# A DeltaNet + gated-GELU kernel: weight conversion that masks two pieces ahead, a new order of the second weight, wider matrix products and fills in the last solve steps

## The chip, the cores and the metric

The kernel runs on one core of one Trainium2 chip. The kernel uses five engines, with a queue of instructions each: TensorE (PE, matrix products; its weight loads are shown apart as PEld), VectorE (DVE), ScalarE (ACT), GpSimd (POOL) and SyncE (SP, which here only issues DMAs). DMAs move data between HBM (DRAM) and the on-chip memory SBUF; products are written to tiles in PSUM. The metric is the device time of one execution in microseconds (us).

## The reference

Four batches of eight heads, 768 tokens, head size 48. A delta rule runs over the tokens and its output, with the heads side by side, is the input of a two-layer block:

```python
k_n = k / (np.linalg.norm(k, axis=-1, keepdims=True) + 1e-06)
for t in range(S):
    y[:, :, t] = np.einsum('bhd,bhde->bhe', q[:, :, t], state)
    v_old = np.einsum('bhde,bhd->bhe', state, kt)
    state = state + bt[:, :, :, None] * np.einsum('bhd,bhe->bhde', kt, vt - v_old)
x = y.transpose(0, 2, 1, 3).reshape(B * S, H * D)          # 3072 x 384
h = x @ w_in                                               # 384 x 2048
out = (h * (1.0 / (1.0 + np.exp(-1.702 * h)))) @ w_out     # 2048 x 384
```

The two weights arrive in double precision (8 bytes a number); the kernel turns them into single precision itself, word by word.

## The kernel before

The tokens are cut into chunks of 128. Inside a chunk the recurrence becomes a triangular system: the Gram matrix of the keys, its diagonal 32x32 blocks inverted on VectorE (`invert`), and four block rows solved one after the other. The first chunk of all four batches (steps 0 to 3, class `Step`) is handled by `hops`: for a pair of steps a and b, eight hops alternate between "solve a block of one step" (`solve`, PSUM tile psU) and "carry the solved block to the blocks below it in the other step" (`below`, PSUM tile psV). After each hop ScalarE copies psU and then one block of psV back to SBUF (tile VU), and the next hop's products wait for both copies. `path` is the hops of steps 0 and 1, `later` those of steps 2 and 3. `put_out` then forms the outputs and the state of a step; its VectorE addition writes ST. `merge` widens 16-row inverses to 32 rows. From step 4 on (class `Half`, called from `slot`) a step has half a chunk of two batches.

The feed-forward block of two batches follows as `hidden` (tile ph, product with w_in, then the activation on ScalarE into gT) and `written` / `both_written` / `seven` (tile po, product with w_out). From step 4 on these products are mixed with the steps by `spend`, and in `later` by `feed`.

The order of each engine's queue is the order in which the Python code emits instructions (`pinned`, line 139 in the profile: nearly every instruction has this line, so tiles tell them apart). Four generators are woven in by hand:

- `conversion` turns one piece of a weight into single precision. Its six instructions are, in order: mask (VectorE, exponent bits of the high words into the destination), clamp (ScalarE), or (VectorE, adds the sign), hi (VectorE, mantissa bits), lo (VectorE, adds the low words), mul (VectorE, the final product into the destination).
- `pieces` lists the pieces: 0 to 3 are halves of the first two quarters of w_in, 4 to 6 and 7 to 9 the thirds of its last two quarters (called (2,0) to (3,2) below, 128x512 each), then the 16 row blocks f of w_out in the order of `order`, with f = 4, 5 and f = 6, 7 taken together.
- `conversions` strings them together. Before the change a piece's mask and clamp are emitted after the hi of the piece before it.
- `background` interleaves the conversions with the inversion of the second chunk, which begins when the eighth row block of w_out is done. `fill(us)` emits from it until the costs that it yields reach that many microseconds.

The raw thirds of w_in are fetched by `fetch_in` on SP's queue. `paced` lets such a fetch wait for a solved block: POOL copies one word of it into the fetch's destination. `fetches` tells which raw row blocks of w_out are fetched once a piece has been converted, since their room becomes free then: some rooms are inside the tile w_out itself (`inside`), the others are buffers of other tiles (`outside`).

`warm(n)` puts n products without use on PE (tile ps_warm), of 128x128 by 128x256 in bf16. They stand at the start, between the products of the first chunk, and in the hops of `path`.

Of the kernel before, what the change touches and what calls it, by code (L numbers as in the profile page):

```python
# [8 lines left out]
F32 = mybir.dt.float32  # L9
# [9 lines left out]
def kernel(  # L19
# [21 lines left out]
    B, H, S, D = q.shape  # L41
    DM, DFF = moe_w_in.shape
# [5 lines left out]
    KC = DM // 128  # L48
    FC = DFF // 128
    BS = 32  # L50
    NB = C // BS
    HB = 2
# [8 lines left out]
    NQ = DFF // 4  # L61
# [8 lines left out]
    ps_moe = ctx.enter_context(tc.tile_pool(name="ps_moe", bufs=2, space=PSUM))  # L70
# [80 lines left out]
    vec, act, pe, pool = Engine(nc.vector), Engine(nc.scalar), Engine(nc.tensor), Engine(nc.gpsimd)  # L151
# [16 lines left out]
    ones = ident.bitcast(mybir.dt.bfloat16)  # L168

    def warm(n, after=None):  # L170
        ps = ps_moe.tile([128, 256], F32, tag="moe", name="ps_warm")
        if after is not None:
            after(ps[:, 0:1], 0.0)
        for _ in range(n):
            pe.matmul(ps, lhsT=ones[:, 0:128], rhs=ones, start=True, stop=True)

    table = cpool.tile([128, 1], F32, name="table")
    act.activation(table, ident[:, 0:1], ACT.Gelu_apprx_sigmoid)
# [41 lines left out]
    def fetch_in(i, other=None, js=None, only=None):  # L220

        f = slice(i * NQ, (i + 1) * NQ)
        for j in range(KC) if js is None else js:
            dst = as_rows(thirds[(i - 2) * KC + j])[:, 0] if i >= 2 else as_rows(quarter(i))[:, j]
            for p, r, m, step in x_rows:
                if only is not None and p // DP != only:
                    continue
                (other if other and (p >= DP or js) else sync)(
                    out=dst[p : p + m], in_=moe_w_in[r + j * step : r + j * step + m, f]
                )  # L230

    places, slots = {}, {}
    inside = {3: 6, 4: 8, 5: 10, 6: 12, 7: 14, 12: 14, 13: 10}
    outside = {0: "xT", 8: "xT", 11: "xT", 1: "M", 9: "M", 14: "M", 2: "M2", 10: "M2", 15: "M2"}
    order = [0, 4, 5, 1, 3, 2, 6, 7, 8, 13, 9, 10, 12, 11, 14, 15]

    def fetch_out(f, dma=sync):

# [10 lines left out]
    def conversion(dst, raw, shape):  # L249

        lo, hi = raw[:, :, :, 0], raw[:, :, :, 1]
        ts, stt = vec.tensor_scalar, vec.scalar_tensor_tensor
        AND, OR = ALU.bitwise_and, ALU.bitwise_or
        E1 = 1 << 20
        p = dst.bitcast(I32)
        ts(p, hi, 0x7FF * E1, None, op0=AND)  # L260
        yield 0.75
        act.activation(p, p, ACT.Relu, scale=8.0, bias=low)
        yield 0.0
        stt(out=p, in0=hi, scalar=-(1 << 31), in1=p, op0=AND, op1=OR)
        yield 0.95
        ts(hi, hi, E1 - 1, E1, op0=AND, op1=OR)
        yield 0.7
        f = lo.bitcast(F32)
        stt(out=f, in0=lo.bitcast(U32), scalar=2.0**-32, in1=hi, op0=ALU.mult, op1=ALU.add)
        yield 0.95  # L270
        stt(out=dst, in0=f, scalar=2.0**-20, in1=dst, op0=ALU.mult, op1=ALU.mult)
        yield 0.95
# [27 lines left out]
    def conversions():  # L300

        whole = list(pieces())

        def begin(i):
            dst, raw, shape, name = whole[i]
            ops = conversion(dst, places[name[1]] if raw is None else raw, shape)
            return ops, next(ops)

        after, cost = begin(0)
        next(after)  # L310
        yield cost
        for i in range(len(whole)):
            ops = after
            yield next(ops)
            yield next(ops)
            if i + 1 < len(whole):
                after, cost = begin(i + 1)
                yield cost
                next(after)
            yield next(ops)  # L320
            cost = next(ops)
            done.add(whole[i][3])
            fetches.pop(whole[i][3], lambda: None)()
            yield cost
# [22 lines left out]
    def fill(us):  # L347
        while us > 0:
            us -= next(behind, us)

    ready = {}
    inverse = {}
# [217 lines left out]
    def send_blocks(n, others=(), dma=sync):  # L570

        G = ready[n][2]
        Nd = dram.tile([H * C * BS], F32, tag="Nd", name="Nd", bufs=4)
        to = Nd.rearrange("(h p k) -> p h k", p=C, k=BS)
        for blk in range(NB):
            u = slice(blk * BS, (blk + 1) * BS)
            k = u if n < B else slice(blk % 2 * BS, (blk % 2 + 1) * BS)
            (beside if blk in others else dma)(out=to[u], in_=G[u, :, k])
        return Nd

    def load_diagonals(Nds):

        for b in range(B):
            load_diagonal(b, Nds[b], sync)
# [88 lines left out]
    def merge(pair, area, banks):  # L673

        XT, Pm = (
            [area[:, a + i * n : a + (i + 1) * n].rearrange("p (h k) -> p h k", h=H) for i in range(HB)]
            for a, n in ((0, H * BS), (HB * H * BS, H * BS // 2))
        )
        Z, HS = [inverse[X.n] for X in pair], BS // 2
        rows = [slice(k * BS, (k + 1) * BS) for k in range(NB)]  # L680
        for X, t in zip(Z, XT):
            vec.transpose(t.rearrange("p h k -> p (h k)"), X.rearrange("p h k -> p (h k)"))
        for X, x, m in zip(pair, Z, Pm):
            ps = banks[0][0].tile([128, H, HS], F32, tag=banks[0][1], name="psP")
            for h in range(H):
                for r in rows:
                    pe.matmul(
                        ps[r, h, :], lhsT=X.G[r, h, r], rhs=x[r, h, HS:], start=True, stop=True,
                        skip_group_check=True,
                    )  # L690
            act.activation(m, ps, ACT.Copy, scale=upper)
            yield
        for x, t, m in zip(Z, XT, Pm):
            ps = banks[1][0].tile([128, H, HS], F32, tag=banks[1][1], name="psZ")
            pe.matmul(ps, lhsT=ident, rhs=x[:, :, HS:], start=True, stop=True, skip_group_check=True)
            for h in range(H):
# [16 lines left out]
    class Step:  # L713
# [69 lines left out]

        def below(self, blk, h, psR):
            r = slice(blk * BS, (blk + 1) * BS)
            for k in range(blk + 1, NB):
                u = slice(k * BS, (k + 1) * BS)
                pe.matmul(
                    self.psV[u, h, :], lhsT=self.G[r, h, u], rhs=self.U[r, h, :],
                    start=False, stop=True, skip_group_check=True,  # L790
                )
# [420 lines left out]
    def run(work):  # L1212
        for _ in work:
            pass
# [161 lines left out]
    ahead_of(inverting, 1 + BS // 2 - 1)  # L1376
    next(inverting)
    run(inverting)
    for b in range(HB, B):
        load_values(b, sync)  # L1380
    pair = [new_step(n) for n in range(B)]
# [15 lines left out]
    def paced(sign, i, j):  # L1397

        words = thirds[(i - 2) * KC + j]
        pool.tensor_copy(words[0:1, 0, 0:1, 0].bitcast(F32), sign)  # L1400
        fetch_in(i, js=(j,))
# [5 lines left out]
        warm(NM)  # L1407
    next(products)
    warm(NM)
    paced(inverse[0][0:1, 0, BS // 2 : BS // 2 + 1], 2, 0)  # L1410
    next(scaling)
    turn(B)
    run(products)
# [11 lines left out]
    def put_out(s, us=1.7):  # L1425
        s.queries()
        s.outputs(True, lambda: fill(us))
        steps.pop(s.n)

    path, later = hops(*pair[:2]), hops(*pair[2:])  # L1430
    for i in range(2 * NB):
        together(*next(path))
        if i in (0, 1, 2, 4, 6):
            at = pair[i % 2].US[i // 2 * BS : i // 2 * BS + 1, 0:1]
            paced(at, *{0: (2, 1), 1: (2, 2), 2: (3, 0), 4: (3, 1), 6: (3, 2)}[i])
        if i == 0:
            warm(NU // 2)
            run(scaling)
        if i in (0, 3, 5):
            turn(B + {0: 1, 3: 2, 5: 3}[i])  # L1440
        if i in (2, 4, 6):
            gram(B + i // 2 - 1)
        if i < 2 * NB - 1:
            warm(NU if i == 1 else NU // 2 if i else 2 * NU // 3)
        if i < 2 * NB - 2:
            fill(2.1)
    put_out(pair[0], 0)
    fetch_out(0, other_queue)
    merging = merge(pair[2:], area, ((ps_big, "big"), (ps_big, "big")))
    put_out(pair[1], 0)  # L1450
    for f in (1, 2):
        fetch_out(f, other_queue)
# [28 lines left out]
    for i in range(2 * NB):  # L1481
        if i == 0:
            for _ in range(HB):
                feed()
                next(merging)
                fill(1.5)
        together(*next(later))
        if i == 1:
            gram(B + HB + 1)
            load_diagonals([send_blocks(n) for n in range(B, 2 * B)])  # L1490
        feed()
        fill(2.3)
    for s in pair[2:]:
# [100 lines left out]
```

## Time and profile before

| | |
|---|---|
| median of 3 runs | 689.9 us (687.72 to 691.27) |
| profiled execution | 696.56 us |
| its span | 694.8 us (1.8 us lie around it) |
| mean granted TensorE clock | 0.972 |
| PE | 670.7 us busy, 9161 products and 9161 weight loads |
| DVE | 474.4 us |
| ACT | 232.0 us |
| POOL | 272.0 us |

The profiled execution is 6.7 us longer than the median of the runs. Times in the text are microseconds from the start of the span. The profile's view by stretches gives each engine's busy time and count of instructions, then the granted clock of TensorE (1.00 is full speed), the mean busy share of the DMA engines and GB/s. In the view in order of time, the bracket at the end of a row is the idle time of the engine ahead of it and what ended that.

### The profile page before, as it was taken

The numbers are of one execution on the slowest core, as the hardware profiler recorded it, in microseconds if no ns is written. First come the engines' busy times: TensorE is split into PE (matmuls) and PEld (weight loads), VectorE is DVE, ScalarE is ACT, GpSimd is POOL, SyncE is SP. The second block draws the span as 40 slices with busy tenths as digits, with TensorE's granted clock in tenths as the row PEclk, the third lists the DMA queues.
The fourth block names the chain that finished last, engine by engine and source line by source line (L and its number), as shares of the span: only waits on it lengthen the run. The fifth ranks groups of instructions, "written<-read, shape, count | busy, mean of one in ns | idle before, by whom it ended". The sixth has DMA issues, their size and how long they took to land.

```text
span 694.8 us, 21515 instructions
## 1 busy us (share of the span) xinstructions
PE 670.7 (97%) x9161; PEld 579.7 (83%) x9161; DVE 474.4 (68%) x888; ACT 232.0 (33%) x563; POOL 272.0 (39%) x290
## 2 busy tenths in 40 slices
PE   9599999998999999999999999999999999999997
PEld 7477878874568898998998998988988988989997
DVE  4787167999688999796997996997995980200000
ACT  3345445552323323323333233233233233232120
POOL 6040084531148751752643734634414305205041
PEclk9679599999999999999999999999999999999999
DMA  8995366647234435336226324335231130000101
GB/s 171 145 172 124 86 144 201 126 73 156 70 85 97 79 73 110 63 69 131 59 49 133 79 61 104 80 63 98 63 66 36 37 66 10 19 13 5 27 0 24
DMA packets 158528, 56.70 MB, mean 82 GB/s; under 512 B 146464, under 2 KB 151296, under 8 KB 158432
## 3 DMA queue, kind: packets, MB, share of 16 engines
q1 hardware_dynamic: 153888, 47.80, 34.3%
q0 software_dynamic: 3456, 7.40, 4.4%
q8 instruction: 72, 1.18, 0.7%
q10 hardware_dynamic: 1088, 0.13, 0.1%
q14 instruction: 24, 0.20, 0.1%
HBM read 39.42 MB, written 14.68 MB: 78 GB/s over the span
## 4 chain that ended last, share of the span: by engine, by line
PE 81%; DVE 6%; DMA 4%; issue 3%; SPq 2%; POOL 2%; ACT 1%; POOLq 0%; DVEq 0%; ACTq 0%
PE ph L139 31%; PE po L139 30%; PE four L139 7%; PE ps_warm L139 4%; PE psU L139 3%; SPq L139 2%; PE psR L139 2%; DVE P L139 2%; DMA KN<-in_k_dram 2%; PE psG L139 1%; DVE w_out L139 1%; DVE YB L139 1%; DMA bL<-in_beta_dram 1%; DVE NT L139 1%; DMA NT<-Nd 1%
## 5 line engine op out<-in xcount | busy, mean ns | idle before, releaser
L139 PE MATMUL ph<-xT,w_in 128*128 128x256 f32 x1152 | 259.8, 383 | 0.9 <-DMA xT<-last 0.9
L139 PEld LDWEIGHTS ph<-xT,w_in 128*128 128x128 f32 x1152 | 215.4, 190 | 31.6 <-DMA xT<-last 1.3
L1063 POOL TENSOR_TENSOR gT<-gT 128x512 f32<-128x512 f32 x80 | 103.2, 1300 | 98.7 <-ACT gT L139 66.0
L139 PE MATMUL po<-w_out,gT 128*128 128x192 f32 (+1 forms) x720 | 138.6, 348 | 0.7 <-DVE w_out L139 0.7
L139 PEld LDWEIGHTS po<-w_out,gT 128*128 128x128 f32 x720 | 118.4, 190 | 12.1 <-DVE w_out L139 1.3
L139 DVE TENSOR_TENSOR P<-NT,YB 64x8 f32<-64x8 f32 (+13 forms) x195 | 124.4, 638 | 5.6
L139 ACT ACTIVATE gT<-ph 128x512 f32<-128x512 f32 x90 | 53.7, 597 | 154.4 <-PE ph L139 153.7
L139 DVE TENSOR_REDUCE YB<-P 64x4 f32<-64x8 f32 (+13 forms) x195 | 78.4, 402 | 6.7
L139 PE MATMUL po<-TW,gT 128*128 128x192 f32 x480 | 81.8, 328 | 0.0
L139 PEld LDWEIGHTS po<-TW,gT 128*128 128x128 f32 x480 | 78.1, 190 | 0.7
L929 POOL TENSOR_SCALAR_AFFINE_SELECT M<-M 64x512 f32<-64x512 f32 x40 | 29.8, 745 | 88.3 <-ACT M L139 87.0
L139 ACT COPY VU<-psU 32x384 f32<-32x384 f32 x96 | 45.0, 469 | 27.7 <-PE psU L139 16.6
L139 DVE TENSOR_TENSOR o<-o,late 128x192 f32<-128x192 f32 x20 | 6.5, 355 | 68.0 <-ACT late L139 67.9
L139 DVE TENSOR_TENSOR VU<-VU,psR 32x384 f32<-32x384 f32 x40 | 22.1, 554 | 32.6 <-PE psR L139 31.8
L366 POOL TENSOR_TENSOR rn<-ssq,half 128x8 f32<-128x8 f32 x12 | 22.4, 1865 | 50.4 <-DVE ssq L139 50.4
L139 PEld LDWEIGHTS psU<-VU,XB 32*32 32x32 f32 x1536 | 29.6, 107 | 13.1 <-issue 8.5
L109 POOL DMA_DIRECT2D KN<-in_k_dram x24 | 17.2, 717 | 59.0 <-PE four L139 35.9
L139 ACT COPY o<-po 128x192 f32<-128x192 f32 (+1 forms) x44 | 14.7, 333 | 75.6 <-PE po L139 73.5
L139 DVE TENSOR_TENSOR VU<-VU,four 128x384 f32<-128x384 f32 x19 | 10.4, 548 | 42.7 <-ACT M L139 42.5
L139 PE MATMUL ps_warm<-ident 128*128 128x256 bf16 x225 | 35.6, 314 | 2.8 <-POOL low L139 1.4
L139 PE MATMUL psU<-VU,XB 32*32 32x48 f32 x1536 | 34.9, 206 | 1.5 <-DVE w_out L139 1.4
L139 PEld LDWEIGHTS <-ident 128*128 128x128 bf16 x225 | 23.8, 111 | 10.1 <-issue 3.0
(165 smaller groups left out, 775.5 us busy)
## 6 DMA issues: line engine op xcount, KB each, us to landing
VU<-in_v_dram SPq DMA_DIRECT2D x40, 96.0 KB, 3.1
out_dram<-o SPq DMA_DIRECT2D x40, 96.0 KB, 2.2
QW<-in_q_dram SPq DMA_DIRECT2D x76, 48.0 KB, 2.2
Kd<-KN SPq DMA_DIRECT2D x56, 64.0 KB, 2.2
late<-Kd SPq DMA_DIRECT2D x14, 256.0 KB, 2.9
NT<-Nd SPq DMA_DIRECT2D x24, 128.0 KB, 3.0
Yd<-NT SPq DMA_DIRECT2D x24, 128.0 KB, 2.3
XB<-Yd SPq DMA_DIRECT2D x24, 128.0 KB, 3.1
```

The lines of the kernel that those rows point to most:

```text
L109: dma(out=place(dst, n)[rows, :, 0:D], in_=src[b, :, t, :].rearrange("h p d -> p h d"),)
L139: return lambda *a, **kw: tc.keep_in_program_order(op(*a, **kw))
L366: nc.gpsimd.tensor_tensor(rn, ssq, half, op=ALU.pow)
L929: nc.gpsimd.affine_select(out=M, in_=M, compare_op=ALU.is_gt, fill=0.0, base=0, pattern=[[0, H], [1, CH]], channel_multiplier=-1,)
L1063: (engine or nc.gpsimd).tensor_tensor(o, a, b, op=op)
```

## The change

Six things change, all of them in or for the first 125 us of the program.

1. Dummies: `warm(n)` issues n // 2 products of 128x512 (the same 256 columns read twice) and one of 128x256 if n is odd.
2. Products: `below` of a `Step` covers the blocks 2 and 3 with one product of 64 rows of output, so that a step has 4 products a head in place of 6.
3. Conversion: the mask of a piece is emitted up to two pieces ahead where its destination does not overlap raw data that is still needed (`clear`), and its clamp one piece ahead.
4. The order of w_out's row blocks; the new order holds both for the conversion and for `both_written`.
5. Fetches: (2,0) of w_in is no longer paced; (2,1) takes its place behind `merge`, and the others follow at hops 0, 1, 3 and 5 rather than 0, 1, 2, 4 and 6.
6. Fills: `fill(2.1)` also in hops 6 and 7 and `fill(2.0)` between the two `put_out`s. The Gram blocks of steps 4 and 5 are sent to DRAM in hops 5 and 6, not all together in `later`.

```diff
     def warm(n, after=None):
-        ps = ps_moe.tile([128, 256], F32, tag="moe", name="ps_warm")
+        ps = ps_moe.tile([128, 2, 256], F32, tag="moe", name="ps_warm")
...
-        for _ in range(n):
-            pe.matmul(ps, lhsT=ones[:, 0:128], rhs=ones, start=True, stop=True)
+        twice = ones.rearrange("p (o k) -> p o k", o=1).broadcast_to([128, 2, 256])
+        for _ in range(n // 2):
+            pe.matmul(ps, lhsT=ones[:, 0:128], rhs=twice, start=True, stop=True)
+        if n % 2:
+            pe.matmul(ps[:, 0], lhsT=ones[:, 0:128], rhs=ones, start=True, stop=True)
...
-    order = [0, 4, 5, 1, 3, 2, 6, 7, 8, 13, 9, 10, 12, 11, 14, 15]
+    order = [0, 1, 3, 4, 5, 2, 6, 7, 8, 9, 13, 12, 10, 14, 11, 15]
...
+        def span(i, raw):
+            kind, f = whole[i][3]
+            if kind == "in":
+                return (4 * NQ, 6 * NQ) if raw and f == 4 * KC - 1 else (0, 0)
+            m = whole[i][2][0]
+            if not raw:
+                return f * DM, (f + m) * DM
+            return (inside[f] * DM, (inside[f] + 2 * m) * DM) if f in inside else (0, 0)
+        def clear(i, j):
+            lo, hi = span(j, False)
+            return all(hi <= a or b <= lo for a, b in (span(k, True) for k in range(i, j)))
...
-        after, cost = begin(0)
-        next(after)
-        yield cost
-        for i in range(len(whole)):
-            ops = after
+        last = len(whole) - 1
+        yield begin(0)
+        clamp(0)
+        yield begin(1)
+        for i in range(last + 1):
+            ops = begun[i]
             yield next(ops)
+            clamp(i + 1)
             yield next(ops)
-            if i + 1 < len(whole):
-                after, cost = begin(i + 1)
-                yield cost
-                next(after)
+            if i < last and i + 1 not in begun:
+                yield begin(i + 1)
+                clamp(i + 1)
+            if i + 2 < last and clear(i, i + 2):
+                yield begin(i + 2)
             yield next(ops)
...
-            for k in range(blk + 1, NB):
-                u = slice(k * BS, (k + 1) * BS)
+            for a, b in {0: ((1, 2), (2, 4)), 1: ((2, 4),), 2: ((3, 4),)}[blk]:
+                u = slice(a * BS, b * BS)
...
     run(inverting)
+    fetch_in(2, js=(0,))
     for b in range(HB, B):
         load_values(b, sync)
...
-    paced(inverse[0][0:1, 0, BS // 2 : BS // 2 + 1], 2, 0)
+    paced(inverse[0][0:1, 0, BS // 2 : BS // 2 + 1], 2, 1)
...
-        if i in (0, 1, 2, 4, 6):
+        if i in (0, 1, 3, 5):
             at = pair[i % 2].US[i // 2 * BS : i // 2 * BS + 1, 0:1]
-            paced(at, *{0: (2, 1), 1: (2, 2), 2: (3, 0), 4: (3, 1), 6: (3, 2)}[i])
+            paced(at, *{0: (2, 2), 1: (3, 0), 3: (3, 1), 5: (3, 2)}[i])
...
-        if i < 2 * NB - 2:
-            fill(2.1)
+        if i > 4:
+            Nds.append(send_blocks(B + i - 5)) if i < 7 else None
+        fill(2.1)
     put_out(pair[0], 0)
...
+    fill(2.0)
     put_out(pair[1], 0)
...
-            load_diagonals([send_blocks(n) for n in range(B, 2 * B)])
+            load_diagonals(Nds[B:] + [send_blocks(n) for n in (B + HB, B + HB + 1)])
```

In the built program the queue of PE holds the same products in the same order, but for the dummies (225 become 117) and the products of `below` (64 fewer); 18322 products and weight loads become 17850.

More of the change, by code (lines that the diff above doesn't have):

```diff
@@ L170, in warm @@
     def warm(n, after=None):
-        ps = ps_moe.tile([128, 256], F32, tag="moe", name="ps_warm")
+        ps = ps_moe.tile([128, 2, 256], F32, tag="moe", name="ps_warm")
         if after is not None:
-            after(ps[:, 0:1], 0.0)
-        for _ in range(n):
-            pe.matmul(ps, lhsT=ones[:, 0:128], rhs=ones, start=True, stop=True)
+            after(ps[:, 0, 0:1], 0.0)
+        twice = ones.rearrange("p (o k) -> p o k", o=1).broadcast_to([128, 2, 256])
[3 more added lines that the diff above has]
+            pe.matmul(ps[:, 0], lhsT=ones[:, 0:128], rhs=ones, start=True, stop=True)
     table = cpool.tile([128, 1], F32, name="table")
@@ L302, in conversions, with clamp @@
         whole = list(pieces())
+        def span(i, raw):
[9 more added lines that the diff above has]
+            return all(hi <= a or b <= lo for a, b in (span(k, True) for k in range(i, j)))
+        begun, clamped = {}, set()
         def begin(i):
             dst, raw, shape, name = whole[i]
-            ops = conversion(dst, places[name[1]] if raw is None else raw, shape)
-            return ops, next(ops)
-        after, cost = begin(0)
-        next(after)
-        yield cost
-        for i in range(len(whole)):
-            ops = after
+            begun[i] = conversion(dst, places[name[1]] if raw is None else raw, shape)
+            return next(begun[i])
+        def clamp(i):
+            if i in begun and i not in clamped:
+                clamped.add(i)
+                next(begun[i])
+        last = len(whole) - 1
[4 more added lines that the diff above has]
+            ops = begun[i]
             yield next(ops)
+            clamp(i + 1)
             yield next(ops)
-            if i + 1 < len(whole):
-                after, cost = begin(i + 1)
-                yield cost
-                next(after)
+            if i < last and i + 1 not in begun:
[3 more added lines that the diff above has]
+                yield begin(i + 2)
             yield next(ops)
```

## The prediction

> **What bounds the kernel now.** I read the page's busy times and slices first. PE is busy for 670.7 of 694.8 us, so the end moves only by what PE loses or by its clock.
>
> ```profile
> PE 670.7 (97%) x9161; PEld 579.7 (83%) x9161; DVE 474.4 (68%) x888; ACT 232.0 (33%) x563; POOL 272.0 (39%) x290
> PE   9599999998999999999999999999999999999997
> DVE  4787167999688999796997996997995980200000
> PEclk9679599999999999999999999999999999999999
> ...
> q8 instruction: 72, 1.18, 0.7%
> ```
>
> The clock falls twice, at 20 to 45 us (nothing of the change is there but a few dummies) and in slice 4, where DVE falls to a tenth too. So I asked for stretches: six around the hops, then the rest of the program.
>
> ```profile
> 61.80:65.20 3.40, 3.40 (x128) 2.73 (x128) 2.76 (x5) 2.75 (x7) 0.43 (x2) 1.00 0.86 221
> 65.20:68.60 3.40, 2.03 (x58) 1.44 (x52) 2.45 (x6) 2.29 (x5) 0.00 (x0) 1.00 0.91 174
> 68.60:72.00 3.40, 3.40 (x86) 2.92 (x86) 1.71 (x3) 1.70 (x5) 0.17 (x1) 0.50 0.17 31
> 75.40:78.80 3.40, 3.40 (x69) 2.67 (x68) 0.00 (x0) 1.07 (x4) 0.46 (x2) 0.50 0.00 0
> 82.30:85.70 3.40, 3.40 (x42) 3.40 (x44) 0.36 (x1) 0.81 (x3) 0.00 (x0) 0.51 0.32 70
> 85.70:89.10 3.40, 3.40 (x157) 2.70 (x153) 2.13 (x5) 1.17 (x4) 1.52 (x4) 1.00 0.07 17
> 150.00:180.00 30.00, 25.80 (x199) 15.44 (x198) 28.98 (x59) 7.88 (x15) 5.59 (x7) 1.00 0.52 113
> 180.00:694.00 514.00, 510.12 (x6882) 454.37 (x6881) 343.36 (x616) 151.91 (x376) 208.55 (x188) 1.00 0.30 63
> ```
>
> From 68.6 to 85.7 PE runs at half clock. From 180 on it is full and untouched. Between 150 and 180 PE is idle for 4.2 us while DVE is full. The waits and the order of time say why (PE's rows, then DVE's, then DVE's waits):
>
> ```profile
> 68.11 0.50 PE L139 MATMUL ps_warm<-ident 128*128 128x256 bf16 x3 [1.37 <-issue]
> 164.42 0.87 PE L139 MATMUL psU<-VU,XB 32*32 32x48 f32 x32 [1.38 <-DVE w_out L139]
> 170.55 0.27 PE L139 MATMUL psR<-VU,G 32*32 32x48 f32 x2 [1.19 <-ACT VU L139]
> 179.06 3.04 PE L139 MATMUL po<-w_out,gT 128*128 128x384 f32 x8 [0.68 <-DVE w_out L139]
> ...
> 84.97 0.36 DVE L139 TENSOR_TENSOR ST<-psY,ST 128x192 f32<-128x192 f32 x1 [11.03 <-ACT xT L139]
> 104.33 0.56 DVE L139 SCALAR_TENSOR_TENSOR w_out<-raw,w_out 128x384 int32<-128x384 int32 x1 [3.74 <-ACT w_out L139]
> ...
> DVE ST L139 <- ACT xT L139: 13.5, 3, 11.0
> DVE w_in L139 <- ACT w_in L139: 8.9, 7, 2.1
> DVE w_out L139 <- ACT w_out L139: 7.9, 5, 3.7
> ```
>
> Two things cost PE time here. First, PE pauses for 1.37 us at 66.75 with nothing to wait for, and the clock falls at the end of that stretch. Second, DVE works without a break from 122 to 180 (the second inversion, 127.6 to 159.6, then eight row blocks of w_out), because it stood for 11.0 us behind the state of step 0 and for 16.8 us behind clamps; PE waits for it four times.
>
> **The pause.** The row q8 (packets, MB, share): 1.18 MB in 72 packets is 16.4 KB each, and 18322 PE instructions over 72 are 254 a packet: the queue brings 256 instructions at a time. PE's pauses with "issue" at 53.73, 66.75 and 98.89 lie 3 and 5 times 256 records apart. So they are ends of blocks whose successor was late. The block that ran out at 66.75 began in hop 2 at 63.1: it lasted 3.65 us, its successor took 5.0 us, with the DMAs 0.86 to 0.91 busy. The Trainium skill ("Runtime: NRT & Kernel Launch", Instruction fetch mechanics) has the same blocks of 256, but calls their cost mostly hidden. The three pauses disagree.
>
> **The parts.**
>
> *Dummies.* 225 become 117 with the same columns. The pitch of the 256-wide ones is 0.11 us (66.25, 66.36, 66.47), so six take 0.66 and three wide ones 0.66 if width is all. The other end is po's pitch, 0.345 for 384 columns (4.14 for 12) or 0.46 for 512: 1.38 for three, +0.7 a hop, over 7 hops 5. po is in f32 and a dummy in bf16, so I take 0.
>
> *Products of `below`.* Hop 1 with three products a head and step takes 0.81 us (60.53 to 61.34), hop 3 with two 0.80. Price 0, between -0.1 and 0.1 a hop.
>
> *The block ends.* 472 instructions fewer put the block ends at the start of hop 2, late in hop 4 and in hop 6. At 2.2 us a hop (60.53, 62.76, 64.96) a block then lasts 4.8 us, against 5.0 for its successor: a pause of 0.2, not 1.37. With that the clock stays up. Hops 4 to 7 start at 68.54, 72.42, 76.17 and about 80.0, and the addition of step 1's state at 86.93. At full clock hop 4 starts at 67.2 and hop 7 at 73.8; the 6.9 us from there hold 4.2 us of PE's output products at half clock (81.46 to 85.67), so 4.8 to 4.9 are left: 78.7. **PE is 8.2 us earlier** (bounds: 0 if the clock falls again; 1.2 if the clock falls but the pause goes).
>
> *DVE in the hops.* The thirds now land earlier: in the profile 5.2 to 6.3 us after their release (55.6 to 60.9; 62.2 to 68.5). So the masks stand at 61, 65, 68.6, 72 and 76. Each clamp is queued on ACT ahead of a hop's copies (hop 3, 5, 6 and behind hop 7's): those come at 66, 69.5, 71.5 and 75, so margins are 2.5 us or more. The 11.0 us are filled: three pieces' work, and the state of step 0 finds DVE at most 1 us late. The extra 2.1 us of mul, lo and or between the two states delay that of step 1 by 0 to 1 us; the first ph waits 0.9 us for xT's DMA there anyway.
>
> *SP and POOL.* SP gets eight Nd DMAs (0.45 us each, 3.6) ahead of xT's; it is idle from 80.2 to 86.9 before, and would end at about 76.6 against xT at 77. The four of (2,0) put the values of steps 2 and 3 off by 1.8 us; these are first read at 88. POOL loses one copy. Price 0, at most 1.
>
> *The order of w_out.* Row block 1 comes by POOL's queue behind `put_out`; its raw DMA takes 4.7 us to land, so 86 at best. Row block 3 needs the room of (3,2), so its DMA starts at about 88 and lands 5.0 to 7.0 us later (raw and w_out rows of the DMA view), 93 to 95.5; but its mask now stands before lo of block 0. DVE waits there for some 5 us, a new stall. Behind it on ACT is the clamp, and behind that the copy of `later`'s hop 2, at 102.8 before and 94.6 after: delay 0 to 1.6, I take 0.5. The pair 6, 7 may cost DVE 2 us more. From there I lay DVE's rows end to end (0.56, 0.36, 0.55, 0.56 a block, 0.96, 0.70, 0.95, 0.96 a pair): the inversion starts at 114 to 116, against 127.6 - 8.2 = 119.4 if nothing but the clock had changed. DVE is thus 3.4 to 5.4 us ahead of PE at 150 to 180, more than any of PE's waits.
>
> *PE's waits.* 0.52, 0.74, 1.38, 1.19, 0.23 and 0.68 at 148 to 179 make 4.74. The first two are ACT's scaling; I leave 0.7 of them: **4.0 us go**.
>
> **Sum.** -8.2 - 4.0 + 0.5 = -11.7 against the profiled execution: 696.56 - 11.7 = 684.9. That execution is 6.7 above the median of the runs. The half clock alone is worth 8.2, and 696.56 - 8.2 = 688.4 lies within the runs' 687.72 to 691.27; so I think that the runs mostly have no such fall. They then gain only 3.5: 689.9 - 3.5 = 686.4. I take the middle, **685 us**, 682 to 688 by itself. About 0.5% (3.4 us) is what a measurement can tell from no change: under 686.5 is faster, over 693.3 slower.
>
> **Rivals.**
> - *The runs had the half clock too*, and the profile adds 6.7 everywhere. For it: an added cost is as good an account of 6.7; against it: the match above. Then 689.9 - 11.7 = 678.
> - *Gain eaten by the late raw blocks.* DVE's stall for row block 3 grows beyond the 5 us that I have; from 9 us on DVE has no lead left, PE's waits come back, and ACT holds hop 2 for 4. Then 689.9 - 4.0 + 4.0 = 690. For it: the 7.0 us row; against it: DMA share falls after 96.
> - *Slower: the last hops are too thin for the clock.* At 68.6 to 82.3 PE shows itself busy all the time, with dummies, and the clock stays at 0.50 for four stretches of 3.4 us; in the last hops a step has one or two products a head. If the clock falls in every run because of the hops' own content, or the new clamps on ACT hold a hop for over 1 us, the runs that were free of it pay 8.2 from hop 4 on, 9.8 from hop 3: 686 + 8 = 694. It decides if a stretch of the hops leaves PE idle for a third (1.37 of 3.4 did). Against it: 58.4 to 65.2 has the same content and kept 1.00. The Trainium skill ("TensorE: Matmul & The Clock Gate", the table at its end) warns of idle gaps over about 3 us only. By that 1.37 us was not the cause, and this rival holds; that the clock falls just at the end of the stretch with the gap speaks for the gap.
>
> **Chances.** Forecast 0.50 (of it 0.38 under 686.5), the runs with half clock 0.17, eaten 0.15 (0.12 same), slower 0.18 (0.15 beyond 693.3). Faster 0.38 + 0.17 = 0.55; same 0.12 + 0.12 + 0.03 = 0.27; slower 0.18. The range takes in 678 and stops at 692.5, which leaves out most of the slow case.
>
> **What would show it.** Right: clock 1.00 from 46 us on; hops 4 to 7 at 2.2 us; DVE's wait before ST under 2 us; PE's waits for DVE w_out gone; the inversion's NT at 114 to 116. Wrong: 0.50 in any stretch of 60 to 85; a pause of over 1 us in the hops; ACT's copies of VU behind a clamp; a wait of DVE for raw or w_out DMAs over 8 us.

## The result, and the profile after

The changed kernel takes **749.19 us** (median; 746.89 to 750.97), the kernel before, on the same chip, 688.81 (687.27 to 691.27): a ratio of 1.0871 [1.0819, 1.0923]. It is 60 us slower, where 5 us faster was forecast; none of the rivals came near. The profiled execution has a span of 749.1 us.

The page's busy times and slices of the changed kernel:

```profile
span 749.1 us, 21043 instructions
...
PE 712.3 (95%) x8925; PEld 594.2 (79%) x8925; DVE 478.6 (64%) x888; ACT 231.2 (31%) x563; POOL 272.4 (36%) x289
PE   9445998999999999999999999999999999999997
DVE  4269424427995889979969979699796894010000
PEclk9685658659999999999999999999999999999999
```

DVE, ACT and POOL are busy for about as long as before. PE has 41.6 us more busy time with 236 matmul records fewer, two slices (2 and 3, counted from 0) in which it is half idle where it was full before, and a granted clock of 0.5 to 0.8 from slice 1 up to slice 8, 168 us, where before it was full from slice 5 on. So two things happened, one ahead of the hops and one in them.

**Ahead of the hops.** The order of time, DVE's and PE's rows with waits, and last the inversion's first row before:

```profile
43.52 0.69 DVE L139 TENSOR_SCALAR w_in<-w_out 128x768 int32<-128x768 int32 x1 [18.29 <-DMA w_out<-in_moe_w_in_dram]
45.98 1.22 DVE L139 TENSOR_TENSOR NT<-NT,bN 128x1024 f32<-128x1024 f32 x1
63.99 1.05 PE L139 MATMUL psP<-XB,gT 32*32 32x16 f32 x64 [15.86 <-DMA XB<-Yd]
...
28.75 1.22 DVE L139 TENSOR_TENSOR NT<-NT,bN 128x1024 f32<-128x1024 f32 x1
```

DVE's queue stands 18.29 us at a mask of w_in whose raw data (quarter 1, in the tile called w_out) has not landed; SP issues it at 35.49 to 38.43, at the same time as before (from 35.45). The first inversion, queued behind it, starts at 45.98; before it started at 28.75. PE gets to the first product with the inverse at 63.99, 14.2 us later than before (49.76).

**In the hops.** ACT's copies of psU end the solves of one hop each. Shown are those of the first and last hop of the first and of the second pair of steps, then PE's rows for one head of hop 1 and the first of the next head, then the same of the kernel before (copies of the first pair, and a head at 60.98):

```profile
75.41 0.47 ACT L139 COPY VU<-psU 32x384 f32<-32x384 f32 x1 [0.64 <-PE psU L139]
115.25 0.47 ACT L139 COPY VU<-psU 32x384 f32<-32x384 f32 x1 [2.19 <-PE psU L139]
131.82 0.47 ACT L139 COPY VU<-psU 32x384 f32<-32x384 f32 x1 [0.37 <-PE psU L139]
173.36 0.47 ACT L139 COPY VU<-psU 32x384 f32<-32x384 f32 x1 [0.48 <-PE psU L139]
...
77.81 0.23 PE L139 MATMUL psU<-VU,XB 32*32 32x48 f32 x1
77.81 0.23 PE L139 MATMUL psV<-VU,gT 32*32 32x48 f32 x1
77.87 0.20 PE L139 MATMUL psU<-VU,XB 32*32 32x48 f32 x1
77.88 0.44 PE L139 MATMUL psV<-VU,gT 32*32 32x48 f32 x3
78.25 0.23 PE L139 MATMUL psU<-VU,XB 32*32 32x48 f32 x1
```

```profile
58.56 0.47 ACT L139 COPY VU<-psU 32x384 f32<-32x384 f32 x1 [0.65 <-PE psU L139]
81.62 0.47 ACT L139 COPY VU<-psU 32x384 f32<-32x384 f32 x1 [2.19 <-PE psU L139]
...
60.98 0.20 PE L139 MATMUL psU<-VU,XB 32*32 32x48 f32 x1
60.98 0.21 PE L139 MATMUL psV<-VU,gT 32*32 32x48 f32 x3
61.02 0.20 PE L139 MATMUL psU<-VU,XB 32*32 32x48 f32 x1
61.03 0.21 PE L139 MATMUL psV<-VU,gT 32*32 32x48 f32 x3
61.06 0.20 PE L139 MATMUL psU<-VU,XB 32*32 32x48 f32 x1
```

The eight hops of the first pair take 39.8 us from the first copy to the last (58.56 to 81.62 before, 23.1), those of the second 41.5 (96.72 to 114.45, 17.7). A head, two records for each of its three products (the last row joins records of both widths), comes every 0.44 us (77.81, 78.25), and this at full clock; with the products of before a head's eight records came every 0.09 us (60.98, 61.06). And the clock falls (PE, PEld, DVE, ACT, POOL, clock, DMA share, GB/s by stretch):

```profile
75.00:80.00 5.00, 5.00 (x56) 3.26 (x53) 3.87 (x6) 1.67 (x3) 0.32 (x1) 1.00 0.44 107
85.00:90.00 5.00, 5.00 (x64) 3.37 (x61) 0.00 (x0) 1.52 (x5) 0.00 (x0) 0.50 0.02 4
90.00:100.00 10.00, 10.00 (x52) 6.03 (x51) 2.75 (x5) 2.13 (x4) 0.17 (x1) 0.50 0.20 52
100.00:110.00 10.00, 10.00 (x102) 6.35 (x104) 2.89 (x6) 4.26 (x9) 0.81 (x2) 0.50 0.07 20
150.00:160.00 10.00, 10.00 (x51) 6.77 (x50) 1.12 (x2) 2.36 (x4) 0.00 (x0) 0.50 0.01 5
```

From 85 on the records leave no gap on PE, and yet it handles 5 to 13 records a us and is granted half the clock. (The end of a product's record is modelled, so the records don't show that the array itself works all that time.) The account against the trace of before: 14.2 us at the first inversion and 2.6 more up to the first copy, at half clock; 16.8 and 23.8 in the two sets of hops, 1.5 between them. The last copy is thus 58.9 us later (173.36, 114.45), and 4.6 are made up behind it, where PE's waits of before are gone: a span that is 54.3 longer.

### The profile page after: what moved, and what is told of

The parts are those of the page before. It is cut to its first block, busy times and chain, and to the rows that moved or that the text cites. A ratio compares the mean times of both kernels' runs of the same rounds, so it can differ in the third digit from the quotient of the medians.

```text
span 749.1 us, 21043 instructions
## 1 busy us (share of the span) xinstructions
PE 712.3 (95%) x8925; PEld 594.2 (79%) x8925; DVE 478.6 (64%) x888; ACT 231.2 (31%) x563; POOL 272.4 (36%) x289
## 4 chain that ended last, share of the span: by engine, by line
PE 93%; SPq 2%; DVE 2%; DMA 1%; issue 1%; ACT 0%; POOL 0%; ACTq 0%; DVEq 0%; POOLq 0%
PE ph L139 35%; PE po L139 31%; PE four L139 7%; PE psU L139 6%; PE ps_warm L139 4%; PE psV L139 3%; SPq L139 2%; PE psR L139 2%; PE psG L139 2%; PE psY L139 1%; DMA w_out<-in_moe_w_in_dram 1%; DVE P L139 1%; DVE YB L139 1%; PE psT L139 1%; PE psZ L139 1%
## 5 line engine op out<-in xcount | busy, mean ns | idle before, releaser
L139 PE MATMUL ph<-xT,w_in 128*128 128x256 f32 x1152 | 266.5, 390 | 0.1
L139 PEld LDWEIGHTS ph<-xT,w_in 128*128 128x128 f32 x1152 | 219.5, 193 | 32.3 <-PE ps_warm L139 0.6
L139 PEld LDWEIGHTS psU<-VU,XB 32*32 32x32 f32 x1536 | 34.7, 109 | 21.3 <-issue 11.3
L139 PE MATMUL psU<-VU,XB 32*32 32x48 f32 x1536 | 50.0, 211 | 0.0
L139 PE MATMUL ps_warm<-ident 128*128 128x512 bf16 x117 | 37.7, 464 | 1.4 <-POOL low L139 1.4
L139 DVE TENSOR_TENSOR VU<-VU,four 128x384 f32<-128x384 f32 x19 | 10.4, 550 | 41.5 <-ACT M L139 41.3
L139 DVE TENSOR_TENSOR P<-NT 64x512 f32<-64x512 f32 (+7 forms) x45 | 31.0, 689 | 1.2
```

Of the source, the lines that this page charges most:

```text
L139: return lambda *a, **kw: tc.keep_in_program_order(op(*a, **kw))
```

## The experiments

Theory: the loss is the sum of two mistakes, the products of `below` with 64 rows of output (32*64 in the profile's rows) between those with 32 (32*32), and the mask of piece 2 issued ahead of the first inversion. Ratios are to the kernel before on the same chip.

**Each undone alone, and both.** First `below` as before:

```diff
-            for a, b in {0: ((1, 2), (2, 4)), 1: ((2, 4),), 2: ((3, 4),)}[blk]:
-                u = slice(a * BS, b * BS)
+            for k in range(blk + 1, NB):
+                u = slice(k * BS, (k + 1) * BS)
```

> The changed kernel with the products of `below` one 32-row block each again; all else as changed. Theory (two causes that add up: the products of 64 rows slow the eight hops that have them, and the mask of piece 2 holds DVE for 18.3 us): the hops get back 16.8 us (psU copies of hop 0 and hop 7 39.8 us apart, 23.1 before) and 23.8 us (41.5 against 17.7), so 749.2 - 40 = 709; PE still waits some 14 us for XB. Rival (the hops are slow because the clock is at one half, whatever the products): at most the 8 to 10 us of a clock fall change, 740.

Measured 704.4 us, 1.0205 [1.0143, 1.0267]: 44.8 us of the 60 are the products, 5 more than expected. Then only the mask, which now isn't issued ahead for piece 2 while piece 0 is at work:

```diff
-            if i + 2 < last and clear(i, i + 2):
+            if 0 < i and i + 2 < last and clear(i, i + 2):
```

> The changed kernel, but the first piece does not mask two ahead, so that the mask of piece 2 no longer stands ahead of the first inversion. Theory: the 14.2 us by which the first merge product starts later (63.99 against 49.75) go, 749.2 - 14 = 735; DVE's wait for w_out<-in_moe_w_in of 18.3 us is gone. Rival (the wait is covered by the slow hops behind it): 745 or more.

Measured 727.3, 1.0537 [1.0475, 1.0599]: 21.9 us off, where 14 were expected. The first copy of psU stands at 58.81 again, for 75.41; the hops still take 37.3 us in both sets, for 39.8 and 41.5. Then both edits:

> The changed kernel with both undone: narrow products in `below` and no mask of piece 2 ahead of the first inversion. Theory: what is left of the change does what the prediction summed, 685 (682 to 688); the hops at 2.2 us and full clock. Rival (the rest of the change is worth nothing or loses, by a clock that falls in the hops or raw blocks that land late): 689 to 694.

Measured 688.84, 0.9982 [0.9949, 1.0015]: the whole loss is gone (60.4; the two alone sum to 66.7, for with the narrow products the mask is worth 15.6, from 704.4 to 688.84). But what is left of the change shows no gain clear of the noise (the interval goes from 3.5 us less to 1.0 more), so the rival came nearer than my 685. Both questions, why the products cost so much and why the rest gains nothing, went on.

**The products alone**, added to the kernel before:

```diff
-            for k in range(blk + 1, NB):
-                u = slice(k * BS, (k + 1) * BS)
+            for a, b in {0: ((1, 2), (2, 4)), 1: ((2, 4),), 2: ((3, 4),)}[blk]:
+                u = slice(a * BS, b * BS)
```

> The kernel before with the 64-row products of below alone. Theory (a product on a 32x64 tile between products on 32x32 tiles costs PE about 0.36 us a head at full clock, whatever stands around it): the copies of psU from hop 0 to hop 7 take about 40 us for the first pair of steps and about 41 for the second, as in the changed kernel, against 23.1 and 17.7 before; the clock falls to 0.50 in both stretches; the first inversion starts near 29 as before; about 689 + 40.6 to 45 = 730 to 734. Rival (the products are slow only together with the later start and the new order of DVE's and SP's work around them): under 700.

Measured 741.82, 1.077 [1.0736, 1.0804], 52.5 us slower; the hops take 41.3 (60.31 to 101.58) and 42.9 us (120.03 to 162.95), with a clock of 0.50 at 66 to 102 and at 126 to 152. So the products do it without the rest of the change. My figure was 8 us low, because I had set it against a profile of before with half clock in its hops. Against the second profile of before (below), whose hops take 17.0 and 17.9 us, the products add 24.3 and 25.0.

**By the number of changes between the tile sizes.** In the hops of blocks 0 and 1 each head goes from the 32-row solve (and product) to the 64-row product and back: 16 changes of size for 8 heads. Issued by kind, with m for the product's width, there are two:

```diff
             for a, b in {0: ((1, 2), (2, 4)), 1: ((2, 4),), 2: ((3, 4),)}[blk]:
+                if psR not in (None, b - a):
+                    continue
...
             for (X, blk), psR in zip(belows, psRs):
-                X.below(blk, h, psR)
+                if psR is not None:
+                    X.below(blk, h, psR)
+        for m in (1, 2):
+            for h in range(H):
+                for (X, blk), psR in zip(belows, psRs):
+                    if psR is None:
+                        X.below(blk, h, m)
```

> The changed kernel with the same products, but within a hop all products of 32 rows are issued first and those of 64 rows behind them, where the changed kernel alternates head by head. Theory (each change between a 32x32 and a 32x64 product makes PE run empty, at 0.36 to 0.5 us a head): 16 changes a hop become 2, most of the 40 us goes, 709 to 715. Rival (a product of 64 rows is slow by itself): no change, 745 to 749.

Measured 720.05, 1.0432 [1.0367, 1.0497], 5 us above the theory's range and far below the rival's. The control has the same grouping and only 32-row products:

> The changed kernel with the 32-row products of before, issued in two groups a hop (first all heads' psU, then all heads' psV): the control for the grouped run, which had 720. Theory (most of what the grouped run still lost is the grouping itself, since products that follow each other then lie in the same row group): 712 to 718, hop 0 of a pair takes over 3 us in the copies of psU, as in the grouped run. Rival (grouping is free, and the 15 us left were the few tile switches that the grouped run still had): 703 to 706, hops of 2.1 to 2.7 us.

Measured 706.87, 1.0249 [1.0216, 1.0282], so it was nearly as the rival had it: grouping itself costs some 2.5 us (704.4 without it; the intervals overlap), and the 13 us left in the grouped run belong to the 64-row products and their two changes a hop. A part of the 13 is clock: in the second set the grouped run has 0.56 at 113 to 120 and 0.66 at 120 to 126, the control 1.00. The order of time of hops 1 and 3 of the grouped run, then of hop 1 of the control, all at full clock (each last row of a hop holds what is left of its psV):

```profile
78.52 0.73 PE L139 MATMUL psU<-VU,XB 32*32 32x48 f32 x13
79.22 1.77 PE L139 MATMUL psV<-VU,gT 32*32 32x48 f32 x29
...
86.08 0.86 PE L139 MATMUL psU<-VU,XB 32*32 32x48 f32 x16
86.88 1.13 PE L139 MATMUL psV<-VU,gT 32*64 32x48 f32 x16
```

```profile
78.08 0.73 PE L139 MATMUL psU<-VU,XB 32*32 32x48 f32 x13
78.75 0.75 PE L139 MATMUL psV<-VU,gT 32*32 32x48 f32 x40
```

Sixteen 64-row records in a row take 1.13 us, 0.07 each; sixteen 32-row ones that all stand on one tile (psU) take 0.86, 0.05 each; forty 32-row ones that turn over three groups of columns take 0.75, 0.02 each. So a wide product takes little longer than a narrow one that has its tile for itself; what the narrow ones of `below` have ahead is that they turn over several tiles. And a mixed group takes 1.77 us for 29 (the name of a row is that of its first record). The third point, two heads at a time, 8 changes a hop:

```diff
+        for g in range(0, H, 2):
+            for m in (0, 1, 2):
+                for h in (g, g + 1):
+                    if m < 1:
+                        for X, blk in solves:
+                            X.solve(blk, h, psU)
+                    for (X, blk), psR in zip(belows, psRs):
+                        if psR is None and m > 0:
+                            X.below(blk, h, m)
+                        if psR is not None and m < 1:
+                            X.below(blk, h, psR)
```

> The changed kernel, its products of a hop issued for two heads at a time: psU and the 32-row psV of both, then the 64-row psV of both. A hop with both tile sizes then changes from one to the other 8 times instead of 16; in the grouped run it was 2. Theory (each change of the tile size costs PE a fixed time, 0.36 us a head for the two): linear in the changes, 720 + 29.1 x 3/7 = 732.5, taken as 730 to 735. Rival (the cost lies in the 64-row products themselves, which the grouping only hides where all heads stand together): 742 to 750.

Measured 736.32, 1.0688 [1.0617, 1.0758], just outside 730 to 735 and clear of the rival. So 16, 8 and 2 changes a hop give 749.2, 736.3 and 720.0 us, and 32-row products alone 704 to 707. Most of the cost (29 us) goes with the changes, the smaller part (13 us) with the wide products themselves and the few changes left. It is not a fixed time for each change: 8 fewer took off 12.9 us, the next 6 fewer 16.3. Both parts hold the clock that falls along with them (a mean of 0.928, 0.945 and 0.967 in the three profiles), which the series does not separate. That PE drains at a change isn't visible in a row. The Trainium skill says it ("TensorEngine Tiling (Array Packing)", Key Properties: "Mode switching requires drain"), and this series agrees with it, though it does not tell a drain from another cost of a change.

**Was the profile of before a usual one?** The same kernel, profiled again:

> The kernel before once more, for its profile alone. Theory (the profile of before was an execution with a late block of instructions, most have none): span 686 to 690, clock 1.00 from 46 us on, no pause of PE over 0.5 us with nothing to wait for between 60 and 80. Rival (the half clock in 68 to 86 is there in every execution): span about 694, 0.50 in four stretches again.

It took 688.29 us, with a span of 686.6. Its clock by slices, then two of the stretches in which the recorded profile had 0.50, then PE's pauses at 50 to 80 with nothing to wait for:

```profile
PEclk9799999999999999999999999999999999999999
```

```profile
68.60:72.00 3.40, 2.98 (x78) 2.38 (x71) 2.35 (x5) 3.30 (x8) 0.17 (x1) 1.00 0.45 122
75.40:78.80 3.40, 3.15 (x84) 2.86 (x87) 0.36 (x1) 1.59 (x6) 0.00 (x0) 1.00 0.96 247
```

```profile
53.87 0.43 PE L139 MATMUL psZ<-P 32*32 32x16 f32 x29 [1.09 <-issue]
67.13 0.50 PE L139 MATMUL ps_warm<-ident 128*128 128x256 bf16 x3 [0.40 <-issue]
71.85 0.60 PE L139 MATMUL ps_warm<-ident 128*128 128x256 bf16 x4 [0.42 <-issue]
```

At 60 to 80 there are two pauses of 0.40 and 0.42 us for one of 1.37, and no fall of the clock. One of 1.09 us stands at 53, at the place where the recorded profile has 0.29, and the clock stays at 1.00 behind it as well; so a pause of about a us is not enough for the fall, and what made the clock fall in the recorded profile stays open. Nor is it of that execution alone: two of the 29 runs of the kernel before beside the last experiments have its span and mean clock (695.1 at 0.972 and 694.9 at 0.971, for 694.8 at 0.972), though they have no profile.

**Why the rest gains nothing.** Against this profile, with both parts undone: the second inversion starts at 117.76 (119.40) and its last product with bL 2.3 us earlier (147.77, 150.10), PE's waits for DVE at 150 to 180 are gone (2.05 us, and 1.7 of lost clock: twelve products of po that took 5.83 us at 157.03 take 4.14), and yet a copy of psU stands at 190.37 in the one and 190.35 in the other, and both spans are 686.6. The reason is that PE comes to the psQ products ahead of these waits 4.1 us later (144.06, 139.95). The gain is lost twice on the way. First, DVE and then ACT with both undone:

```profile
107.69 0.56 DVE L139 TENSOR_SCALAR w_out<-w_out 128x768 int32<-128x768 int32 x1 [5.11 <-DMA w_out<-in_moe_w_out_dram]
...
105.33 0.47 ACT L139 COPY VU<-psU 32x384 f32<-32x384 f32 x1
108.29 0.94 ACT L139 ACTIVATE w_out<-w_out,low 128x768 int32<-128x768 int32 x1 [2.11 <-DVE w_out L139]
109.25 0.47 ACT L139 COPY VU<-psU 32x384 f32<-32x384 f32 x1
```

The mask of the pair 6, 7 waits 5.11 us for its raw data, the clamp waits for the mask, and the copy of hop 7 stands behind the clamp: 3.92 us after hop 6, for 2.01. Second, PE waits for ACT's TW, QS and kT (1.56, 0.65, 0.74 us at 140 to 148), because ACT's scalings of KN just ahead wait for reciprocals that are queued on DVE behind pieces of the inversion. Of these, 0.51 for QS and 0.74 for kT are there before too, so 1.7 us are new. With the 1.9 of hop 7 they make most of the 4.1; hop 6 was 1.1 late already (105.33, 104.22). Three runs tried to take these away one at a time. The normalization of steps 10 and 11 begun three turns earlier:

```diff
-    starts = {2 * B: 1, 2 * B + 1: 9, 2 * B + 2: 6, 2 * B + 3: 8}
+    starts = {2 * B: 1, 2 * B + 1: 9, 2 * B + 2: 3, 2 * B + 3: 5}
```

> Both parts undone, and the normalization of steps 10 and 11 started three turns of the loop earlier (3 and 5 for 6 and 8). In the run with both undone, PE waits 4.4 us for ACT's QS, 1.6 for TW and 0.9 for kT at 140 to 148, and ACT's scalings of KN stand just ahead of them at 134.97, 139.40 and 141.69, the first two released by DVE's reciprocals. Theory (these waits replaced the 4.0 us that went, and moving the scalings ahead takes most of them away): 684 to 686, the waits of PE for QS and TW under 2 us together. Rival (the scalings move but the waits of PE pass on to the second inversion or the next product): 687.5 to 690, as with both undone.

Measured 690.5, 1.0012 [0.9989, 1.0035]: no gain. (The 4.4 us for QS in the expectation are a sum over 20 to 250 us; at 140 to 148 it is 0.65.) Step 9's reciprocal is now the last, at 143.72, and the wait for QS is 2.32. The old order of w_out:

```diff
-    order = [0, 1, 3, 4, 5, 2, 6, 7, 8, 9, 13, 12, 10, 14, 11, 15]
+    order = [0, 4, 5, 1, 3, 2, 6, 7, 8, 13, 9, 10, 12, 11, 14, 15]
```

> Both parts undone, and the order of w_out of before as well. With both undone, DVE waits 4.28 us for row block 3 (92.80) and 5.11 for the pair 6, 7 (107.69); ACT's clamp behind the second (108.29) stands ahead of hop 7's copy of psU (109.25), which comes 3.92 us after hop 6's, against 2.01 in the kernel before. Theory (the late row blocks eat what DVE's head start gives): hop 7 of the second pair at about 2 us, no wait of DVE for a w_out DMA over 3 us, 685.5 to 687.5. Rival (these waits cost nothing at the end, since PE waits for the scalings of KN at 140 to 148 whenever it gets there): 688 to 690.

Measured 693.16, 1.0048 [1.0014, 1.0081]: slower, outside both expectations. The hops did what the theory said (hop 7 2.02 us after hop 6, the inversion at 111.97, 7.4 us ahead of the kernel before), and then PE loses time that it did not lose before. PE's waits and what ACT does, then two stretches:

```profile
138.92 1.56 PE L139 MATMUL ph<-xT,w_in 128*128 128x256 f32 x6 [1.41 <-ACT TW L139]
141.13 1.00 PE L139 MATMUL psQ<-QS,kT 48*64 48x112 f32 x32 [0.65 <-ACT QS L139]
147.93 1.14 PE L139 MATMUL psG<-kT 48*64 48x64 f32 x32 [3.87 <-ACT kT L139]
...
146.29 0.62 ACT L139 ACTIVATE w_out<-w_out,low 128x384 int32<-128x384 int32 x1 [3.46 <-DVE w_out L139]
147.29 0.59 ACT L139 ACTIVATE kT<-psT 128x512 f32<-128x512 f32 x1
```

```profile
145.00:150.00 5.00, 2.07 (x34) 1.65 (x35) 4.86 (x12) 2.75 (x6) 0.94 (x2) 0.72 0.98 199
150.00:155.00 5.00, 5.00 (x11) 2.71 (x10) 4.74 (x13) 1.74 (x3) 0.91 (x2) 0.59 0.74 177
```

With the inversion earlier, the next clamp of w_out slips in on ACT ahead of kT; its mask is queued on DVE behind the inversion's end, so ACT stands 3.46 us and PE 3.87, and the clock falls. In the kernel before that clamp stands behind kT (152.49, kT at 142.97). The eight sends of steps 4 and 5 taken out of hops 5 and 6 as well:

```diff
-        if i > 4:
-            Nds.append(send_blocks(B + i - 5)) if i < 7 else None
...
-            load_diagonals(Nds[B:] + [send_blocks(n) for n in (B + HB, B + HB + 1)])
+            load_diagonals([send_blocks(n) for n in range(B, 2 * B)])
```

> The run with the old order of w_out, and the blocks of steps 4 and 5 sent in the second pair's hops as before, not in hops 5 and 6: eight DMAs fewer on SP ahead of xT's. With both undone, the first ph products wait 0.42 and 0.32 for xT's DMA and take 2.8 us for 1.4; in the kernel before there is no such wait. Theory (my price 0, at most 1, for SP's queue was low): the first hop of the second pair 1 to 1.4 us earlier against the end of the first pair's, 684.5 to 686.5. Rival (the blocks sent late are in the way there as much): as the run with the old order.

Measured 695.09, 1.008 [1.0063, 1.0098]: no help; the way from the first pair's last copy to the second's first is 13.1 us, as without it (13.0), 13.8 with both undone, 12.8 before. So the theory on SP fell. What took the 0.8 is not shown: the stretch itself differs by more between runs whose kernels are the same up to there (13.0 to 14.2 with the old order of w_out, 13.7 to 15.2 with the new).

**Issue order or a full DVE?** In the 25 turns beside the inversion, `fill(1.0)` issues 1 us of DVE's spare work. Less of it puts the reciprocals and masks that ACT needs further ahead in DVE's queue; no work is left out. With both parts undone and the old order of w_out:

```diff
     for i in range(25):
-        fill(1.0)
+        fill(0.8)
```

> Both parts undone, the old order of w_out, and 0.8 us instead of 1.0 of DVE's spare work issued in each of the 25 turns beside the second inversion. With the old order alone, the second inversion starts at 111.97, 7.4 us ahead of the kernel before, and yet PE stands 5.9 us at 135 to 150: 1.41 for ACT's TW and 0.65 for QS behind scalings of KN that wait for DVE's rn, and 3.87 for kT, behind a clamp of w_out that waits on ACT for DVE's mask; the clock falls to 0.72 and 0.59 there. Theory (PE waits there because DVE's queue holds work from ahead of what ACT needs, a matter of issue order and not of DVE's time): with 5 us less ahead of them, the waits shrink to under 2 us, the clock stays up, and the head start shows: 681 to 686. Rival (the scalings wait for DVE whatever the order, since it is full): 690 to 695 as with the old order.

Measured 687.59, 0.9968 [0.9939, 0.9996]: 5.6 us less than with 1.0, which is below the rival's range, though above the theory's. With 0.6:

> The same with 0.6 us a turn: 10 us of DVE's work later in the queue. Theory: the waits for ACT's TW, QS and kT gone, but the second inversion ends up to 10 us later in the queue, at about 147 to 150 as in the kernel before, and PE waits for the products behind it as there (2 to 4 us): 684 to 689, no better than with 0.8. Rival (scalings wait whatever the order): 690 to 695.

Measured **685.19, 0.9927 [0.9894, 0.996]**, 0.7% faster than the kernel before, and better against 0.8 than I expected. The kernel before with 0.6 was not run, so how much of this gain needs the rest of the change stays open. With 0.8 and the new order of w_out:

> Both parts undone, the new order of w_out kept, and 0.8 us a turn. With 1.0, the waits for TW, QS and kT take 2.95 us at 140 to 148. Theory: they go to about 1.5 or less, and 1 to 2 us come off: 685.5 to 688. Rival: 688 to 690 as with 1.0.

Measured 689.13, 0.9988 [0.9962, 1.0015], as the rival had it: the waits for ACT shrink to 1.9 us, but hop 7 is still late (3.78 us) and a wait of 1.67 for DVE's w_out at 172.01 comes back. It is 1.5 us more than with the old order and 0.8. So both the late raw data of the new order and the issue order held the gain back. The stretch that decides, in the runs with 1.0, 0.8 and 0.6 us (old order, one run a fence):

```profile
130.00:150.00 20.00, 14.07 (x145) 10.88 (x144) 19.31 (x38) 11.40 (x38) 6.58 (x5) 0.93 0.56 102
```

```profile
130.00:150.00 20.00, 17.88 (x162) 13.51 (x161) 19.31 (x38) 12.41 (x40) 6.59 (x6) 1.00 0.44 88
```

```profile
130.00:150.00 20.00, 19.26 (x169) 14.73 (x168) 19.27 (x39) 12.64 (x40) 5.24 (x4) 1.00 0.40 76
```

DVE is busy 19.3 of 20 us in all three, so it is the order in its queue, not its load, that PE's 5.93, 2.12 and 0.74 us of idle time depend on.

## Why the prediction was wrong, step by step

- **Products of `below`: "Price 0, between -0.1 and 0.1 a hop"** is the step that failed: 45 us (undone in the changed kernel) to 53 (added to the one before). The rows that I set it by, a hop with three products a head against one with two, all have 32x32 tiles. They price the number of products, and the change was one of size. No row of before has a 32x64 product at all, so the bounds had no row behind them. What the runs showed in its place: the change between the two sizes, 0.44 us a head for 0.09 at full clock, and a clock that falls to 0.50 along with it.
- **The first of the conversion was not in the sum at all.** I followed the masks two ahead into the hops and not to the first inversion, where `clear` lets the mask of piece 2 go ahead because its room is free, and does not ask whether its data have landed. That is 18.3 us of DVE, 21.9 us at the end with the wide products and 15.6 with the narrow ones. Each of the two alone would have made the kernel slower.
- **Dummies, price 0:** held. Two wide ones take 0.59 us (80.46, both undone), four narrow ones 0.60 (80.04, before profiled again).
- **Block ends, 8.2 us:** with both undone the clock is 1.00 from 60 on, PE has no pause over 0.2 us at 60 to 90 with nothing to wait for, and hops 4 to 7 take 2.0 to 2.2; so the rival of hops too thin for the clock fell as well. But the second profile of before has full clock there too, and its hops 4 to 7 take 2.2 to 2.6: "the runs mostly have no such fall" was right, and of the 8.2 about 1 us is left (16.0 us from first to last copy, for 17.0). In the second profile 255 records lie between the pauses of 0.40 and 0.42 us, so they are ends of blocks as well. Beyond 100 us neither profile of before shows such a pause, with some 60 of its 72 blocks there. That is what the Trainium skill's "mostly hidden" says ("Runtime: NRT & Kernel Launch", Instruction fetch mechanics), and I had set it aside for the three that were late.
- **DVE in the hops:** with both undone the masks stand at 62.2, 66.7, 69.4, 73.2 and 78.6 (61, 65, 68.6, 72, 76 forecast) and the 11.0 us gap is down to 2.6, ahead of the last of these masks. Held, but for that last mask.
- **Order of w_out:** a stall of 5 us for row block 3 (4.28 measured) and 2 for the pair 6, 7 (5.11), the inversion at 114 to 116 (117.76), a hop late by 0.5 (1.9, and hop 7, not 2). The mechanism was right, its second term too small.
- **PE's waits, 4.0 us:** those for DVE went, as forecast. In their place came waits for ACT at 130 to 150, 2.95 us with both undone for 1.25, which the profile of before could have told: there too ACT's scalings wait for rn (1.55 and 0.58 us, and 1.54 and 0.59 in the second profile), so they had no room. The rival "gain eaten by the late raw blocks" describes half of it: the stall for row block 3 stayed at 4.28 us, but the pair 6, 7 held a hop. In the changed kernel itself 4.0 us of PE's waits did go, as forecast, but there PE had come 58.9 us later and the inversion 52.6 (180.23 for 127.60): that DVE was ahead of PE is luck, not the mechanism.

## What to carry to other kernels

Fewer instructions are not cheaper if they differ in kind from their neighbours: before merging two small products into a wide one, look for a row in which both sizes alternate, and where there is none, do not call the price 0. Where a queue is reordered, ask of every instruction moved forward whether its data have landed, beginning with the first one, not only whether its room is free. An engine that gets ahead helps only if what others need of it moves ahead in its queue as well; here 0.6 for 1.0 us of spare work a turn was worth 8 us, with the old order of w_out and both parts undone.

## What the runs showed of the hardware that was not expected

A change between 32x32 and 32x64 tiles is dear: 0.44 us a head against 0.09, with three products in place of four. The granted clock fell to 0.50 over 85 to 110 us without a gap in PE's records. The Trainium skill ("TensorE: Matmul & The Clock Gate", the table at its end) warns of idle gaps of over about 3 us, and none stands there, so by the records its rule doesn't account for this fall. Of the first pair's extra time, the last three hops, whose products have the old size, show the clock's share: 11.9 us for 7.0. And two executions of one kernel can differ by a stretch at half clock (spans of 694.8 and 686.6 us), so a sum against a single profile carries that much with it.
